# The order of loads and of row groups at a kernel's start, and later weight loads for its last stage: one change to an attention and mixture-of-experts kernel

## The chip, the cores and the metric

The kernel runs on one core of a Trainium2 chip. The metric is the device time of one execution in microseconds, the median of several runs on the chip. Before the change it is 813.06 us, the median of 3 runs (812.66 to 814.68).

## The reference, cut to what matters

```python
# attention: B, H, S, D = 2, 8, 576, 64
psi_rel = log1p(abs(pos[:, None] - pos[None, :]))
x = (psi_rel / log1p(maximum(pos[:, None], 1)))[..., None]
bias = maximum(x @ w1 + b1, 0) @ w2            # 32 hidden units, one bias per head
attn = softmax(q @ k.T / sqrt(D) + bias)       # over keys
x = (attn @ v) as 1152 rows x 512
# first mixture: 4 experts, all of them, weighted by p
x = sum over e of p[:, e] * (maximum(x @ w1[e], 0) @ w2[e])
# second mixture: 8 experts, one for each row
logits = x @ w_gate; e_idx = argmax(logits)
out[mask] = gate_w[mask] * eom[mask, e] * (maximum(x[mask] @ w1[e], 0) @ w2[e])
```

The bias depends on the query row i, the key j and the head, and not on the batch.

## The kernel before

**Engines and order.** Nothing reorders the program: the whole of it is written under a manual schedule, so each engine (TensorE, VectorE, ScalarE, GpSimd) and each DMA queue runs its instructions in the order in which the Python code issues them. Two queues matter here, SP's, which carries most loads, and POOL's, which carries the routing rows of the last stage. Tiles come from pools with a fixed number of buffers; an instruction that writes a buffer waits until the earlier reader of that buffer is done.

**Attention.** The 1152 query rows are nine units of 128: unit u has batch u % 2 and rows from 128 (u // 2), and the ninth has 64 rows of each batch. A head of a unit is one step n of the long loop, n = 8 u + h, 72 steps, each staggered over several turns: `qk(n)` puts scores of 128x576 into PSUM, `soft_max(n)` (L361, VectorE) adds the bias and takes the row extreme in one pass, `soft_exp(n)` (L371, ScalarE) takes the exponential, `e_trans` transposes it, and `av` multiplies with v. The rows call the pass at L361 by its tiles, ns out of sc and bias. `soft_max(n)` for head 0 needs the complete bias tile of its block.

**Bias.** Two units with the same rows share one block of bias, a tile of 128 rows by 8 heads by 576 keys. A block is made in eight groups T of 16 rows: four times `bias_r` (L305 on VectorE or L310 on ScalarE) makes the 32 hidden units for four rows, 128x576; `bias_mm` multiplies them with w2 on TensorE into PSUM; `bias_out` (L332, ScalarE) takes the result out into a buffer bo of SBUF, and one DMA on SP's queue (L335) scatters it into every eighth row of the bias tile. These buffers come from a pool with two under the name bo; the odd groups of block 0 use those of ns instead.

**Keys and values.** k of a batch comes in three loads (`load_k`, a = 0, 1, 2; 512, 512 and 128 KB), is split into two parts by GpSimd in five pieces (`k_split`), and each piece goes through two sets of transposes (`k_trans`, TensorE, PSUM buffers et shared with the transposed exponentials) and two copies (`k_out`, L217). Batch 0 is needed from head 0 on, batch 1 from head 8 on. v is loaded in three parts of a batch; `v_max` (L246) and `v_pow` (L250 to L253) find a power of two over its largest absolute value, `v_scale` (L258 to L260) spreads it and `v_mul` (L264) scales v by it, after which v is split as well.

**The start.** After the first loads a loop over T = 0 to 8 makes block 0; its list `bulk` names the load that is issued behind each bias row. Then come the loads that are left, and the loop over n from -2, which makes the first two groups of block 1 in its first two turns and the transposed k of batch 1 in its turns -1 to 3.

**From the first experts to the second.** The first mixture's matmuls run in 96 tiles (`l1`, `l2`), while the weights of the second are scaled, split and stored to DRAM (wdr). The second mixture works in slots of 128 rows, each with one expert. `route` computes the logits of three units, writes rows of y with their gate to DRAM (ydr, L897, POOL's queue), and `ids_in` (L1011, POOL's queue) gathers the rows of a slot. For the first three slots this is done early, out of units 0 to 5. A slot s then runs through `x_pre` (L1020 on VectorE, then ScalarE), `x_tr` (transposes), `lay1` (L1048) and `lay2` (L1067). `load_e(w, s)` (L1090, SP's queue) fetches the weights of layer w for slot s in four DMAs of 512 KB, with the expert's number in a register. Two buffers for each layer serve slots s % 2.

## Time and profile before

| | |
|---|---|
| median of 3 runs | 813.06 us (812.66 to 814.68) |
| the profiled execution | 816.86 us |
| its span | 815.1 us |
| TensorE busy | 750.1 us, 92% of the span |
| VectorE, ScalarE, GpSimd busy | 488.5, 476.2, 351.7 us |
| granted TensorE clock, mean over the span | 0.971 |
| DMA, mean | 197 GB/s, 160.21 MB |

The profile is one execution, recorded by the hardware. Its page gives busy times of the engines, the span in 40 slices of equal length, the DMA queues, and the costliest groups of instructions; the trace behind it answers for any stretch, line or tile. A granted clock of 1.00 is 2.4 GHz for TensorE and 0.50 is 1.2 GHz. The DMA share is the mean busy share of the core's 16 DMA engines, and can pass 1 by the way in which packets are counted. All times in rows are microseconds from the start of the span, unless marked ns.

### The profile page before, as it was taken

The numbers are of one execution on the slowest core, as the hardware profiler recorded it, in microseconds if no ns is written. First come the engines' busy times: TensorE is split into PE (matmuls) and PEld (weight loads), VectorE is DVE, ScalarE is ACT, GpSimd is POOL, SyncE is SP. The second block draws the span as 40 slices with busy tenths as digits, with TensorE's granted clock in tenths as the row PEclk, the third lists the DMA queues.
The fourth block names the chain that finished last, engine by engine and source line by source line (L and its number), as shares of the span: only waits on it lengthen the run. The fifth ranks groups of instructions, "written<-read, shape, count | busy, mean of one in ns | idle before, by whom it ended". The sixth has DMA issues, their size and how long they took to land. (4 is left out here: it accounts for less than half of the span.)

```text
span 815.1 us, 16401 instructions
## 1 busy us (share of the span) xinstructions
PE 750.1 (92%) x6303; PEld 481.3 (59%) x6303; DVE 488.5 (60%) x1210; ACT 476.2 (58%) x694; POOL 351.7 (43%) x258
## 2 busy tenths in 40 slices
PE   6477999998889999999999999999999789999994
PEld 3245777776785555555555555555555477667771
DVE  6577999998877546565456565465477373333210
ACT  5557999996855657676667667667662132222220
POOL 8532744452553455545546555555543203112110
PEclk9769999999999999999999999999999899999998
DMA  9912443466274386466647468564537739999340
GB/s 210 217 45 70 94 104 99 124 175 137 49 231 153 155 279 245 181 233 232 257 161 273 163 249 277 194 258 142 202 124 291 303 131 341 409 407 360 117 152 16
DMA packets 73860, 160.21 MB, mean 197 GB/s; under 512 B 18928, under 2 KB 27632, under 8 KB 73778
## 3 DMA queue, kind: packets, MB, share of 16 engines
q1 hardware_dynamic: 67904, 144.38, 52.6%
q0 software_dynamic: 4528, 14.47, 5.3%
q8 instruction: 51, 0.84, 0.4%
q10 hardware_dynamic: 1346, 0.28, 0.2%
q14 instruction: 31, 0.25, 0.1%
HBM read 116.35 MB, written 39.34 MB: 191 GB/s over the span
## 5 line engine op out<-in xcount | busy, mean ns | idle before, releaser
L511 POOL TENSOR_TENSOR ring<-wraw,ring 128x1024 f16<-128x1024 f32 x64 | 136.1, 2128 | 119.0 <-ACT wraw L508 103.2
L735 DVE SCALAR_TENSOR_TENSOR h<-hps,h 128x384 f16<-128x384 f32 x96 | 53.2, 557 | 147.4 <-ACT h L734 147.4
L730 PE MATMUL hps<-xt,wt 128*128 128x384 f16 x384 | 126.1, 328 | 2.3 <-DVE h L735 1.8
L731 PE MATMUL hps<-xt,wt 128*128 128x384 f16 x384 | 126.2, 329 | 0.0
L732 PE MATMUL hps<-xt,wt 128*128 128x384 f16 x384 | 125.9, 328 | 0.0
L476 DVE TENSOR_REDUCE wm<-wraw 128x1 f32<-128x1024 f32 x96 | 115.9, 1209 | 0.0
L508 ACT ACTIVATE wraw<-wraw,wR 128x1024 f32<-128x1024 f32 x91 | 104.5, 1148 | 3.0
L747 PE MATMUL yps<-wt,h 128*128 128x512 f16 x264 | 100.1, 379 | 0.0
L748 PE MATMUL yps<-wt,h 128*128 128x512 f16 x264 | 100.1, 379 | 0.0
L749 PE MATMUL yps<-wt,h 128*128 128x512 f16 x264 | 100.1, 379 | 0.0
L734 ACT ACTIVATE h<-hps 128x384 f16<-128x384 f32 x96 | 46.6, 486 | 89.6 <-PE hps L732 85.4
L511 POOL TENSOR_TENSOR wt<-wraw,wt 128x1024 f16<-128x1024 f32 x31 | 66.1, 2132 | 63.8 <-ACT wraw L508 63.4
L503 ACT ACTIVATE ring<-wraw,wR 128x1024 f16<-128x1024 f32 x64 | 73.0, 1141 | 21.5 <-DVE wR L492 18.8
L1048 PE MATMUL l<-xb,wb 128*128 128x128 f16 x1248 | 72.8, 219 | 1.0 <-ACT o L1071 0.8
L1048 PEld LDWEIGHTS <-wb 128*128 128x128 f16 x1248 | 70.7, 98 | 4.6 <-DMA wb<-wdr 1.2
L352 PE MATMUL sc<-kt,qt 128*128 128x288 f32 x320 | 62.4, 320 | 9.1 <-DVE mn L361 6.6
L1067 PE MATMUL l<-wb,xb 128*128 128x512 f16 x312 | 69.5, 379 | 0.8 <-ACT o L1071 0.8
L305 DVE TENSOR_SCALAR_CACHE_REDUCE r<-lm,nbp 128x576 f32<-128x576 f32 x88 | 67.0, 806 | 1.4 <-PE bp L323 1.3
L361 DVE CUSTOM_DVE_ANT_0 ns<-sc,bias 128x576 f32<-128x576 f32 x72 | 54.3, 754 | 21.5 <-PE sc L352 12.5
L1056 DVE SCALAR_TENSOR_TENSOR xb<-l,xb 128x512 f16<-128x512 f32 x26 | 17.6, 691 | 80.2 <-ACT xb L1055 80.2
L1072 POOL DMA_INDIRECT out_x<-o,g x13 | 13.2, 1017 | 106.7 <-ACT o L1071 92.8
L371 ACT ACTIVATE e<-ns,mn 128x576 f32<-128x576 f32 x72 | 56.5, 784 | 1.2 <-DVE mn L361 1.1
(248 smaller groups left out, 1432.9 us busy)
## 6 DMA issues: line engine op xcount, KB each, us to landing
wb<-wdr SPq DMA_DIRECT2D x104, 512.0 KB
wraw<-in_moe_w SPq DMA_DIRECT2D x84, 512.0 KB
wdr<-ring SPq DMA_DIRECT2D x64, 512.0 KB
bias<-bo SPq DMA_DIRECT2D x32, 288.0 KB
wraw<-in_moe_w POOLq DMA_DIRECT2D x12, 512.0 KB, 5.2
qt<-qt SPq DMA_DIRECT2D x40, 128.0 KB
ydr<-y POOLq DMA_DIRECT2D x9, 258.0 KB, 3.6
bias<-bo SPq DMA_DIRECT2D x16, 144.0 KB
```

Source lines behind the costliest of these rows:

```text
L476: dve.tensor_reduce(out=wm[:, w_col(x), k:k + 1], in_=wraw[x][:, k], axis=AX.X, op=ALU.max, apply_absolute_value=True)
L503: act.activation(out=hi, in_=t, func=AF.Copy, scale=R)
L508: act.activation(out=t, in_=t, func=AF.Copy, scale=R)
L511: pool.tensor_tensor(out=lo, in0=t, in1=hi, op=ALU.subtract)
L730: pe.matmul(ps, lhsT=w[:, k, 0, fs], rhs=xt[:, c, 0, k, :], start=(k == 0), stop=False)
L731: pe.matmul(ps, lhsT=w[:, k, 0, fs], rhs=xt[:, c, 1, k, :], start=False, stop=False)
L732: pe.matmul(ps, lhsT=w[:, k, 1, fs], rhs=xt[:, c, 0, k, :], start=False, stop=(k == 3))
L747: pe.matmul(acc[m][t], lhsT=hh, rhs=w[:, f // 2, 0, ws], start=(f == 0), stop=False)
L748: pe.matmul(acc[m][t], lhsT=hh, rhs=w[:, f // 2, 1, ws], start=False, stop=False)
L749: pe.matmul(acc[m][t], lhsT=hl, rhs=w[:, f // 2, 0, ws], start=False, stop=(f == 7))
L1048: pe.matmul(ps[f // 4][:, f % 4, :], lhsT=w[:, k, a, f * 128:f * 128 + 128], rhs=xs[:, b, k, :], start=(k == 0 and f % 4 == 0 and i == 0), ...
L1067: pe.matmul(ps, lhsT=hs[:, a, f, :], rhs=w[:, f // 2, b, c], start=(f == 0 and i == 0), stop=(f == 7 and i == 2))
```

## The change

At the start, the loads of k for batch 1 leave the place ahead of the first bias row and go behind the first and the second; the load of q for unit 1 goes behind the last bias row; the piece of lm (the logarithms) goes from behind the sixth bias row to behind the third, and the v loads of batch 0 from behind the third to fifth to behind the fourth to sixth; the first v load of batch 1 joins the other two, behind all of block 0. The loop over T runs to 10 and makes groups 0 and 1 of block 1 as well, and it scales the low lm piece itself. The maxima of v, their power of two, the scale and the multiplication come one turn later, behind the first `soft_max`. Three of five pieces of k of batch 1 are transposed and copied ahead of the loop over n, the other two in its first two turns.

At the end, only the first layer's weights of slot 0 are fetched where all four sets of the first two slots were; the other three sets are fetched after the third gather, behind a DMA of 16 bytes that reads the third gathered tile.

```diff
@@ the start
-        for a in (2, 0):
-            load_k(1, a)
...
-        bulk = [lambda: load_k(1, 1), lambda: load_q(1), lambda: load_v(0, 0), lambda: load_v(0, 1), lambda: load_v(0, 2),
-                lambda: sp.dma_start(out=lm[:, 0:448], in_=lmc[:, 0:448]), lambda: None, lambda: load_v(1, 0)]
-        for T in range(9):
+        def load_lm():
+            sp.dma_start(out=lm[:, 0:448], in_=lmc[:, 0:448])
+
+        bulk = [[lambda: load_k(1, 2), lambda: load_k(1, 0)], [lambda: load_k(1, 1)], [load_lm], [lambda: load_v(0, 0)],
+                [lambda: load_v(0, 1)], [lambda: load_v(0, 2)], [], [lambda: load_q(1)]]
+        for T in range(11):
             if 3 <= T < 8:
                 for g in range(2):
                     k_out(0, T - 3, g)
-            if T < 8:
+            if T < 10:
                 for tt in range(4):
-                    bias_r(0, T, tt, "a" if tt in AT[T % 2] else "v")
+                    bias_r(T // 8, T % 8, tt, "a" if tt in AT[T % 2] else "v")
+            if T == 7:
+                dve.tensor_scalar(out=lm[:, 0:448], in0=lm[:, 0:448], scalar1=w1c, scalar2=None, op0=ALU.mult)
             if T == 8:
-                for x in range(2):
-                    v_max(0, x)
-                v_pow(0)
                 qk(0)
             if T:
-                bias_mm(0, T - 1)
-                bias_out(0, T - 1, len(AT[(T - 1) % 2]))
-                bulk[T - 1]()
+                x = divmod(T - 1, 8)
+                bias_mm(*x)
+                bias_out(*x, len(AT[(T - 1) % 2]))
+                for f in bulk[T - 1:T]:
+                    for y in f:
+                        y()
...
-        for a in (1, 2):
+        for a in range(3):
             load_v(1, a)
         sp.dma_start(out=cs[:, C_UT:C_N], in_=cst[:, C_UT:C_N])
-        dve.tensor_scalar(out=lm[:, 0:448], in0=lm[:, 0:448], scalar1=w1c, scalar2=None, op0=ALU.mult)
...
+        k_pass(4, 0, 1)
@@ the loop over n
+            if n == -2:
+                for x in range(2):
+                    v_max(0, x)
+                v_pow(0)
-            if n == -2:
+            if n == -1:
                 v_scale(0)
                 v_mul(0)
...
-            if n < 0:
-                for tt in range(4):
-                    bias_r(1, n + 2, tt, "vavv"[tt])
-            if n == 0:
-                rb[1] = 6
...
             if n < 0:
-                bias_mm(1, n + 2)
-                bias_out(1, n + 2, 1)
+                k_pass(n + 4)
...
-            if -1 <= n < 4:
-                k_pass((4, 0, 1, 2, 3)[n + 1])
@@ from the first experts to the second
             if i == 93:
                 for w in range(2):
                     wbuf(w, 0)
-                    load_e(w, 0)
+                load_e(0, 0)
...
         for w in range(2):
             wbuf(w, 1)
-            load_e(w, 1)
...
                     for s in range(NE):
                         ids_in(s)
+                    sp.dma_start(out=after, in_=sl[NE - 1][0][0:1, 0:4])
+                    load_e(1, 0)
+                    for w in range(2):
+                        load_e(w, 1)
```

SP's queue at the program's start. ks and kraw1 are the k loads of batch 1 (the first ks is batch 0's), bias0 a row group of block 0, qt two copies between partitions, q unit 1's rows, vraw parts of v, lm the piece of logarithms. Before:

```order
L184 DMA ks_131<-in_k 64x8x64
L184 DMA ks_133<-in_k 64x8x64
L188 DMA kraw1_135<-in_k 128x8x128
L335 DMA bias0_168<-bo_188 16x8x576
L188 DMA kraw1_135<-in_k 128x8x128
L173 DMA qt_198<-qt_198 64x512
L174 DMA qt_198<-qt_198 64x512
L335 DMA bias0_168<-bo_215 16x8x576
L139 DMA q_219<-in_q 128x8x64
L335 DMA bias0_168<-bo_247 16x8x576
L230 DMA vraw_251<-in_v 128x4x128 x2
```

The same place on SP's queue after the change:

```order
L184 DMA ks_131<-in_k 64x8x64
L335 DMA bias0_164<-bo_184 16x8x576
L184 DMA ks_188<-in_k 64x8x64
L188 DMA kraw1_190<-in_k 128x8x128
L173 DMA qt_197<-qt_197 64x512
L174 DMA qt_197<-qt_197 64x512
L335 DMA bias0_164<-bo_214 16x8x576
L188 DMA kraw1_190<-in_k 128x8x128
L335 DMA bias0_164<-bo_245 16x8x576
L537 DMA lm_117<-in_lmc 128x448
L335 DMA bias0_164<-bo_275 16x8x576
L230 DMA vraw_279<-in_v 128x4x128 x2
```

Each bias row stands ahead of loads that stood ahead of it, and q of unit 1 is gone from this stretch.

VectorE around the first head's pass (L361, ns). r is a row group's hidden units, vm_112, vmx and vpb the maxima of v and their power of two, lm the piece of logarithms that is scaled. Before:

```order
L305 TENSOR_SCALAR r,rmx<-lm,nbp 128x576 x12
L246 TENSOR_REDUCE vm_112<-vraw 128x1 x2
L250 TENSOR_REDUCE vmx<-vm_112 128x1
L251 TENSOR_SCALAR vmx<-vmx 128x1
L252 TENSOR_SCALAR vmx<-vmx 128x1
L253 CAST vpb<-vmx 128x1
L566 TENSOR_SCALAR lm<-lm,cs 128x448
L361 ISA ns,mn<-sc,bias_168 128x576
L361 ISA mn 128x1
```

VectorE in the same place after the change:

```order
L305 TENSOR_SCALAR r,rmx<-lm,nbp 128x576 x12
L549 TENSOR_SCALAR lm<-lm,cs 128x448
L305 TENSOR_SCALAR r,rmx<-lm,nbp 128x576 x6
L361 ISA ns,mn<-sc,bias_164 128x576
L361 ISA mn 128x1
L246 TENSOR_REDUCE vm_112<-vraw 128x1 x2
L250 TENSOR_REDUCE vmx<-vm_112 128x1
L251 TENSOR_SCALAR vmx<-vmx 128x1
L252 TENSOR_SCALAR vmx<-vmx 128x1
L253 CAST vpb<-vmx 128x1
L305 TENSOR_SCALAR r,rmx<-lm,nbp 128x576
```

Six more hidden-unit rows now stand ahead of the first pass, and the maxima of v behind it.

ScalarE before the loop over n, after the change: bo_425 and bo_439 are the results of the first two groups of block 1, kt1 the copies of transposed k of batch 1.

```order
L332 ACTIVATE bo_425<-bp_414,bconst_98,cs_97 128x288
L332 ACTIVATE bo_425<-bp_415,bconst_98,cs_97 128x288
L332 ACTIVATE bo_439<-bp_429,bconst_98,cs_97 128x288
L332 ACTIVATE bo_439<-bp_430,bconst_98,cs_97 128x288
L217 CAST kt1_121<-ktp_460 128x4x64
L217 CAST kt1_121<-ktp_466 128x4x64
L217 CAST kt1_121<-ktp_472 128x4x128
```

Three more such copies follow in the same manner; before the change, all of these stood between exponentials of the loop over n.

SP's queue where the weights of the first two slots are fetched. wb00 is layer 0 of slot 0, wb10 its layer 1; the instructions between are the register arithmetic for an address. Before:

```order
L1090 DMA wb00_7366<-wdr_4102 128x2048
L1090 ISA
L1090 DMA wb10_7380<-wdr_4102 128x2048
L1090 ISA
L1090 DMA wb10_7380<-wdr_4102 128x2048
```

The same place after the change:

```order
L1090 DMA wb00_7367<-wdr_4103 128x2048
L1182 DMA after_4090<-xg_7489 1x4x1
L1090 ISA
L1090 DMA wb10_7368<-wdr_4103 128x2048
L1090 ISA
L1090 DMA wb10_7368<-wdr_4103 128x2048
```

The 16-byte DMA at L1182 reads xg, the third gathered tile, and everything behind it on SP's queue waits with it.

## Rows read from the trace of the kernel before

**Rows 1.** Page: TensorE's busy tenths in 40 slices; DMA total.

```profile
PE   6477999998889999999999999999999789999994
...
DMA packets 73860, 160.21 MB, mean 197 GB/s; under 512 B 18928, under 2 KB 27632, under 8 KB 73778
```

**Rows 2.** Stretches: us, PE, PEld, DVE, ACT, POOL, PEclk, DMA share, GB/s.

```profile
30.00:41.00 11.00, 0.29 (x1) 0.11 (x1) 3.75 (x7) 2.04 (x4) 1.95 (x2) 0.54 1.09 208
41.01:80.06 39.05, 29.09 (x237) 19.11 (x238) 29.38 (x71) 25.31 (x46) 10.52 (x11) 0.81 0.24 60
```

**Rows 3.** Timeline, VectorE: start, duration, what, [idle before <-releaser].

```profile
35.84 1.35 DVE L246 TENSOR_REDUCE vm<-vraw 128x1 f32<-128x1152 f32 x1 [4.22 <-DMA bias<-bo]
...
37.23 0.15 DVE L250 TENSOR_REDUCE vmx<-vm 128x1 f32<-128x2 f32 x1
...
41.01 0.76 DVE L361 CUSTOM_DVE_ANT_0 ns<-sc,bias 128x576 f32<-128x576 f32 x1 [2.64 <-DMA bias<-bo]
...
43.55 0.81 DVE L305 TENSOR_SCALAR_CACHE_REDUCE r<-lm,nbp 128x576 f32<-128x576 f32 x1
44.28 0.81 DVE L305 TENSOR_SCALAR_CACHE_REDUCE r<-lm,nbp 128x576 f32<-128x576 f32 x1
...
80.06 0.75 DVE L361 CUSTOM_DVE_ANT_0 ns<-sc,bias 128x576 f32<-128x576 f32 x1
```

**Rows 4.** Waits of VectorE, 41.00 to 80.06: us, times, longest.

```profile
DVE ns L361 <- PE sc L352: 3.3, 1, 3.3
DVE ns L361 <- ACT e L371: 2.6, 2, 1.6
DVE vP L258 <- PE vpp L257: 2.2, 1, 2.2
DVE r L305 <- PE bp L323: 1.3, 1, 1.3
```

**Rows 5.** Timeline, DMA issues and times to landing of the gather chain.

```profile
626.60 1.62 POOL L897 DMA_DIRECT2D ydr<-y  x3 [10.43 <-DVE y L895]
637.67 1.10 POOL L1011 DMA_INDIRECT xg<-ydr,ids_e  x1 [9.46 <-DVE oh L849]
...
ydr<-y POOLq DMA_DIRECT2D x4, 258.0 KB, 7.3
ydr<-y POOLq DMA_DIRECT2D x9, 258.0 KB, 3.6
DMA to landing us min/median/max: 3.9/6.5/7.0
...
644.25 0.69 DVE L1020 TENSOR_REDUCE g<-xg 128x1 f32<-128x512 f32 x1 [3.46 <-DMA xg<-ydr,ids_e]
646.79 1.89 PE L836 MATMUL lgp<-wgt,yt 128*128 128x16 f32 x8 [4.95 <-ACT yt L831]
662.57 2.85 PE L1048 MATMUL l<-xb,wb 128*128 128x128 f16 x48
```

**Rows 6.** Stretches of the gather chain and behind, columns as in rows 2.

```profile
640.00:646.00 6.00, 1.84 (x11) 0.87 (x9) 2.19 (x11) 0.65 (x2) 2.06 (x5) 0.95 1.03 405
645.46:652.28 6.82, 5.49 (x21) 3.67 (x22) 2.38 (x17) 1.21 (x3) 0.18 (x1) 0.51 0.18 71
680.00:760.00 80.00, 79.05 (x904) 58.58 (x902) 25.16 (x70) 20.89 (x35) 16.52 (x23) 1.00 0.93 370
```

**Rows 7.** Timeline, SP's queue at the start: issue, duration, what.

```profile
4.60 2.03 SPq L184 DMA_DIRECT2D ks<-in_k  x2
...
12.22 0.60 SPq L335 DMA_DIRECT2D bias<-bo  x1
```

**Rows 8.** DMA view: packets in 12 to 41 us, then 5 to 9.

```profile
DMA packets 8425, 6.13 MB, mean 211 GB/s; under 512 B 1945, under 2 KB 7143, under 8 KB 8423
...
DMA packets 2494, 1.14 MB, mean 284 GB/s; under 512 B 500, under 2 KB 2494, under 8 KB 2494
```

**Rows 9.** Timeline, ScalarE: the copies of one k piece.

```profile
67.86 1.15 ACT L217 CAST kt<-ktp 128x512 fp32r<-128x512 f32 x2 [1.06 <-PE ktp L208]
```

More of the change, by code (lines that the diff above doesn't have):

```diff
@@ L782, in attn_moe_moe_kernel @@
     tab = rt_p.tile([1, 128], I32, name="tab")
+    after = rt_p.tile([1, 4], F32, name="after")
     early = rt_p.tile([1, NE], I32, name="early")
```

## Prediction, made before the changed kernel was run

> **What bounds the kernel now.** I read the page's slices first. TensorE is at 9 tenths or more nearly everywhere; the thin places are the first four slices (to about 80 us), a shallow dip around 200 us, and the two slices from 632 to 672 us [rows 1]. The diff acts in two of them: the start, and the step from the first expert layer to the second.
>
> The table by stretches prices the start [rows 2]. From 30 to 41 us it is busy 0.29 of 11.00 at a granted clock of 0.54, while the DMA share is 1.09 and 208 GB/s move: the DMA engines are full and everything else waits. What it waits for stands in VectorE's rows [rows 3]: the first head's maximum at 41.01 sat 2.64 us for a bias row, because it needs all eight bias rows of block 0. From it to the ninth head's maximum 39.05 us pass (41.01 to 80.06). In that stretch VectorE is busy 29.38 us and TensorE 29.09 at a clock of 0.81 [rows 2]; VectorE's 9.67 idle us are split between score matmuls, exponentials, the v scale and bias matmuls [rows 4].
>
> The second thin place is a chain. The three ydr stores are issued from 626.60; the gathers behind them start only at 637.67, after 9.46 us of waiting; the first gathered rows arrive at 644.25, where VectorE has sat 3.46 us; TensorE, idle 4.95 us for a copy that ScalarE makes behind these rows, goes on at 646.79 [rows 5]. For the next 6.82 us the granted clock is 0.51, that is the 1.2 GHz level, with TensorE busy 5.49. SP's weight loads fill the DMA engines meanwhile: 405 GB/s from 640 to 646 [rows 6].
>
> **The profiled execution against the median.** It took 816.86 us (span 815.1 plus 1.8 around it), 3.80 above the median of 813.06. No term below is a share of the whole, so savings read from it are taken off 813.06 as they stand.
>
> **Part 1, the order of the loads: +1.5 us on the last bias row.** Ahead of the last row of block 0 the change puts 128 + 512 KB of k that before were issued from 4.60 on, ahead of the first bias row at 12.22 [rows 7]. It takes out q of unit 1, 256 KB. The v loads of batch 0 all stay ahead of it, and so does the lm piece; each bias row moves past one v load only. Net 384 KB, 0.39 MB, more before the row that ends the wait. At the mean of 211 GB/s of 12 to 41 us this is 1.9 us, at the 284 GB/s of the k loads 1.4 [rows 8]. I take 1.5. Bounds: -1.2 (q's 0.26 MB at 211 GB/s gone, and the k pieces hidden in a gap) to 3.1 (0.66 MB of k at 211 GB/s with nothing given back). POOL splits these k pieces after all of batch 0, in the order of before, so it comes to them late and I count nothing there.
>
> **Part 2, what fills the wait.** Two bias groups of block 1 go from after the first maximum to before it: 6 instructions on VectorE, each 0.73 from start to start (43.55 to 44.28) [rows 3], 4.4 us less in the stretch. The absolute maxima of v and their power of two go the other way: two reductions of 1.35 (35.84) and four small ones of 0.15 (37.23 is the first) [rows 3], 3.3 us more. Busy time falls from 29.4 to 28.3. The scaling of the low lm piece only moves to an earlier place in the wait.
>
> The groups' two matmul sets, their ScalarE evictions and the copies of three of five k pieces leave the stretch too. A k piece is 8 transposes on TensorE and two ScalarE copies, 1.15 together [rows 9]; two pieces stay, but come before the first transposed exponentials. The matmuls and k copies stand behind a catch: the eviction of the second group writes a buffer from which row 6 of block 0 must first have left. ScalarE waits there until one row before the end, and the six copies queue behind it, with the score matmul of head 1 behind their transposes on TensorE. VectorE covers this: after the first maximum it has the v maxima and one more bias row, 3.3 + 0.7 us of its own.
>
> The idle time in the stretch: of the 9.4 us in [rows 4] the 3.3 for scores (the first k piece and a bias group stood in front of them at 1.2 GHz) should fall to 1, the 2.6 for exponentials to 0.5, the 1.3 for bias matmuls to 0; the v scale of batch 1 keeps about 1.5 of its 2.2, and the same wait for batch 0, which the 30 to 41 us stretch hid, now costs about 1. That is 4.0, an estimate. The stretch becomes 28.3 + 4.0 = 32.3 for 39.05, 6.7 less; minus the 1.5 of part 1: **5.2 us**. Bounds: with 1.0 idle and the same delay 8.2; with all 9.67 idle still there and 3.1 of delay, -2.0 (a loss). Behind the ninth head TensorE stands at 9 tenths [rows 1] and every later stage starts from the heads, so this goes through to the end.
>
> **Part 3, the late weights: 5.0 us.** Three of four weight loads of the first two slots (12 DMAs of 512 KB) leave their place on SP ahead of the gathers and are issued after the third gather has landed, behind a 16-byte DMA that reads it. Without them the stores meet an idle queue: a store takes 7.3 us to land in that stretch, 3.6 over the whole program, and a gather 6.5 in the median where the quickest takes 3.9 [rows 5]. The last store then lands near 632, the gathers are issued at about 632.4, 633.8 and 635.1 (the offsets of before), and land at 636 to 639. VectorE reaches the first at 644.25 - 3.46 = 640.79, so its whole wait goes and the chain behind it, ScalarE and TensorE, moves up by 3.46. What is late next is that chain itself: 2.5 us from VectorE's start to TensorE's (644.25 to 646.79), which leaves TensorE 1.5 idle. With 1.5 instead of 4.95 idle the clock may stay at 2.4 GHz; 5.49 busy us at the lower level are worth at most 2.7, and VectorE's routing steps hold some of it, so 1.5, bounds 0 and 2.7. Sum 3.5 + 1.5 = 5.0, bounds 3.5 and 6.2.
>
> The price of delay: 12 x 0.524 = 6.3 MB at 405 GB/s are 15.5 us from about 639, the end near 655. Slot 1's first layer starts at 662.57 [rows 5] less 5.0 = 657.6; its 2 MB stand second in the queue and have landed by 651. The margin of some 6 us hides the change; SP's next loads wait for TensorE to free their buffers anyway.
>
> A rule speaks against this part: the Trainium skill, page "DMA: Bandwidth & Descriptors", section "Rules for kernel authors", says to issue a DMA early, compute, and wait on its semaphore late. By it, moving 12 loads back by some 15 us would be a loss; the trace shows the other side of it, a gather that lands at 644.25 behind loads that are needed 10 us later. The rule's result is the second rival.
>
> **Rivals.** *The start gives nothing* (chance 0.13): the last rows land 3 us later, ScalarE's wait for the buffer holds the copies, and the first heads idle as before. For it: DMA sets the start, and the change removes only 0.26 MB from it; against it: VectorE's own work covers some 4 us. 813.06 - 5.0 = 808.1.
>
> *The late weights cost what the gather gains* (0.09): the wait for rows becomes a wait for weights in slot 1's first layer. It decides when 4.2 MB from 641 take longer than to 657.6, under 253 GB/s; at the page's mean for the whole program, 197 [rows 1], they take 21 us, TensorE waits near 5 us and part 3 is nil. 813.06 - 5.2 = 807.9. Against it: 405 GB/s in the same stretch with the same DMAs [rows 6].
>
> *The change does not do what it says* (0.06): the rows land 3 later and the waits stay, and weights are late too. Within 2.4 us of 813.1.
>
> *Slower* (0.04): the moved 6.3 MB land in the stage of the slots, where the DMA share is 0.93 from 680 to 760 us [rows 6]. If that queue does not drain before slot 2's weights are due, TensorE waits in slot after slot for up to all that those loads take, 15.5 us: 813.06 - 5.2 - 5.0 + 15.5 = 818. It decides when the part of it that no margin covers passes 12.6 us. Against it: TensorE is busy 79.05 of 80 there, so loads are ahead.
>
> **How the numbers follow.** Forecast (0.68): 5.2 + 5.0 = 10.2 off 813.06, 802.9; alone it spans 799.1 (8.2 and 5.8) to 807. The range 799.0 to 808.4 takes in the first two rivals. A measurement of this kernel tells about 0.3%, 2.4 us, from no change: faster by more is the forecast and two rivals, 0.90; within it 0.06; slower 0.04.
>
> **What would show it.** Right: the first maximum 1 to 3 us after 41.0; the ninth near 75 for 80.06, with VectorE idle 3 to 5 us between them; bias groups of block 1 on VectorE before the first maximum; the first gather issued near 632; no wait of VectorE for it; a granted clock of 1.00 behind it; no wait of the slot matmuls for weights over 1 us. Wrong: a first maximum after 45, an idle sum of 9, a gather still issued after 635, or TensorE waiting for weights at the first layer of slot 1.

## The result, and the profile after

The changed kernel takes 805.57 us, the median of 5 runs (803.55 to 810.10), where the kernel before took 813.06 in 5 runs (811.46 to 814.68). The ratio is 0.9913, interval 0.9888 to 0.9938, that is 5.0 to 9.1 us faster. The forecast was 802.9 in a range of 799.0 to 808.4: the direction and the two main mechanisms held, one term (the clock behind the gather) came only in part, and the size came out 2.7 us too large.

| | before | after |
|---|---|---|
| median | 813.06 us | 805.57 us |
| profiled execution, and its span | 816.86, 815.1 us | 805.57, 803.8 us |
| first and ninth head's pass on VectorE | 41.01, 80.06 us | 42.49, 74.00 us |
| third gather issued, counted from the first ydr store of its three | 640.41 - 626.60 = 13.8 us | 627.82 - 619.75 = 8.1 us |
| last matmul row of the routing chain (L836) | 646.79 us | 636.37 us |

TensorE's busy tenths on the page of the changed kernel, in 40 slices:

```profile
PE   6677999998889999999999999999998989999994
```

Against [rows 1], the second slice went from 4 to 6 tenths, and the thin place near the end from 7 and 8 to 8 and more.

The table by stretches of the changed kernel: us, then busy us (and instructions) of PE, PEld, DVE, ACT, POOL, then granted clock, DMA share, GB/s. The first row is the wait before the first head's pass, the second goes from that pass to the ninth, the third is the end of the routing chain:

```profile
30.00:42.49 12.49, 4.03 (x41) 1.63 (x42) 4.19 (x12) 4.63 (x10) 1.75 (x2) 0.79 1.07 180
...
42.49:74.00 31.51, 23.53 (x203) 18.30 (x204) 28.08 (x67) 22.96 (x41) 10.48 (x11) 0.87 0.42 97
...
637.90:641.40 3.50, 3.50 (x13) 1.83 (x12) 2.12 (x14) 0.59 (x1) 0.00 (x0) 0.51 1.01 392
```

The stretch over the first nine heads is 31.51 us long for 39.05 in [rows 2], and VectorE is busy 28.08 of it for 29.38: its idle time fell from 9.67 to 3.43. The wait ahead of it still moves data at a full DMA share. Here is VectorE around its end, in the timeline (start, duration, what, and in brackets the idle time before it with what ended it):

```profile
28.09 1.48 DVE L549 TENSOR_SCALAR lm<-lm,cs 128x448 f32<-128x448 f32 x1 [0.87 <-DMA lm<-in_lmc]
...
33.37 0.81 DVE L305 TENSOR_SCALAR_CACHE_REDUCE r<-lm,nbp 128x576 f32<-128x576 f32 x1
...
42.49 0.76 DVE L361 CUSTOM_DVE_ANT_0 ns<-sc,bias 128x576 f32<-128x576 f32 x1 [8.30 <-DMA bias<-bo]
...
43.17 2.61 DVE L246 TENSOR_REDUCE vm<-vraw 128x1 f32<-128x1152 f32 x2
...
47.74 0.76 DVE L361 CUSTOM_DVE_ANT_0 ns<-sc,bias 128x576 f32<-128x576 f32 x1 [0.47 <-PE sc L352]
...
74.00 0.75 DVE L361 CUSTOM_DVE_ANT_0 ns<-sc,bias 128x576 f32<-128x576 f32 x1
```

The bias groups of block 1 are done at 34.2, and then VectorE sits 8.30 us for the last bias row: the wait is as much of a wait as before, but it now comes after work that used to come behind it. VectorE's waits between 30 and 80 us (total, times, longest):

```profile
DVE ns L361 <- DMA bias<-bo: 8.3, 1, 8.3
DVE ns L361 <- PE sc L352: 1.3, 2, 0.8
DVE vP L258 <- PE vpp L257: 0.9, 1, 0.9
DVE etl L390 <- ACT eth L384: 0.8, 1, 0.8
```

Against [rows 4], the 3.3 for a score matmul became 1.3 in two, the waits for exponentials and for bias matmuls are gone, and of the 2.2 for the v scale 0.9 is left; a wait of 0.8 for ScalarE's transposed exponentials (L390) is new. ScalarE's timeline shows the catch that the prediction named:

```profile
34.59 1.07 ACT L332 ACTIVATE bo<-bp,bconst,cs 128x288 f32<-128x288 f32 x2 [2.52 <-DMA bias<-bo]
41.01 1.07 ACT L332 ACTIVATE bo<-bp,bconst,cs 128x288 f32<-128x288 f32 x2 [5.35 <-DMA bias<-bo]
41.97 0.65 ACT L217 CAST kt<-ktp 128x256 fp32r<-128x256 f32 x2
```

The two evictions of block 1's groups wait 2.52 and 5.35 us for a buffer, and the first k copy starts only at 41.97.

At the end, the gather chain of the changed kernel, from the timelines of GpSimd, VectorE and TensorE; the third row, from the view of L1011, is the time from a gather's issue to its landing:

```profile
619.75 1.63 POOL L897 DMA_DIRECT2D ydr<-y  x3 [10.58 <-DVE y L895]
625.08 1.11 POOL L1011 DMA_INDIRECT xg<-ydr,ids_e  x1 [3.71 <-issue]
...
DMA to landing us min/median/max: 3.6/3.6/3.6
...
633.84 0.67 DVE L1020 TENSOR_REDUCE g<-xg 128x1 f32<-128x512 f32 x1
...
636.37 1.06 PE L836 MATMUL lgp<-wgt,yt 128*128 128x16 f32 x8 [1.37 <-ACT yt L831]
...
642.05 1.50 PE L1048 MATMUL l<-xb,wb 128*128 128x128 f16 x24
```

In [rows 5] the first gather came 11.07 us behind the stores and VectorE sat 3.46 us for its rows; now it comes 5.33 us behind them, and VectorE does not wait. The profile puts the 9.46 us of [rows 5] down to a VectorE row (L849); that is a coincidence in time, since the same row starts at 630.23 in the changed kernel, 5 us behind the gather. What the gather reads are the rows that the ydr stores write, so the wait is for these stores to land (7.3 us in the median, [rows 5]). TensorE's idle time ahead of L836 fell from 4.95 to 1.37 us. SP's queue in the same stretch shows the DMA of 16 bytes and the weight loads behind it:

```profile
631.46 0.74 SPq L1182 DMA_DIRECT2D after<-xg  x1
632.42 32.02 SPq L1090 DMA_DIRECT2D wb<-wdr  x19
```

### The profile page after: what moved, and what is told of

Read it like the earlier page. It is cut to its first block, busy times and chain, and to the rows that moved or that the text cites. A ratio compares the mean times of both kernels' runs of the same rounds, so it can differ in the third digit from the quotient of the medians.

```text
span 803.8 us, 16406 instructions
## 1 busy us (share of the span) xinstructions
PE 746.6 (93%) x6303; PEld 479.8 (60%) x6303; DVE 489.1 (61%) x1210; ACT 476.7 (59%) x694; POOL 352.2 (44%) x258
## 5 line engine op out<-in xcount | busy, mean ns | idle before, releaser
L361 DVE CUSTOM_DVE_ANT_0 ns<-sc,bias 128x576 f32<-128x576 f32 x72 | 54.3, 754 | 21.7 <-PE sc L352 9.6
```

## The experiments

Each kernel ran beside the kernel before. The first four rows of the table were run on one chip, the next four and the last four on others; the medians of the kernel before there are 814.09, 814.65 and 814.11 us. A ratio is always to the kernel before on the same chip; it is formed from all the runs and is not the quotient of the two medians. Passes and stretches are read from one trace of each kernel.

| kernel | median us | ratio, interval | first, ninth pass us |
|---|---|---|---|
| late weights alone | 810.95 | 0.9944 (0.9919 to 0.9968) | 41.27, 79.23 |
| start alone | 811.19 | 0.9955 (0.9931 to 0.9980) | 42.43, 74.63 |
| whole change, old order of work | 812.08 | 0.9965 (0.9940 to 0.9990) | 42.66, 79.95 |
| whole change, k loads early | 802.30 | 0.9843 (0.9810 to 0.9875) | 38.12, 69.06 |
| whole change, no waiting DMA | 812.29 | 0.9970 (0.9948 to 0.9992) | 42.69, 74.62 |
| whole change, k pieces in the loop | 811.19 | 0.9959 (0.9942 to 0.9976) | 42.21, 79.09 |
| k early, v behind block 0 | 802.36 | 0.9848 (0.9826 to 0.9870) | 34.46, 71.09 |
| whole change again | 806.03 | 0.9891 (0.9869 to 0.9913) | 43.82, 76.22 |
| whole change, bias groups in the loop | 815.42 | 1.0008 (0.9985 to 1.0032) | 42.89, 82.20 |
| k early, k copies first | 800.65 | 0.9833 (0.9808 to 0.9858) | 38.22, 69.05 |
| k early, q and then v behind block 0 | 798.72 | 0.9805 (0.9774 to 0.9836) | 34.53, 67.93 |
| k early again | 801.25 | 0.9837 (0.9811 to 0.9862) | 38.64, 70.89 |

### The two halves apart

Late weights alone: the three hunks at the end, on the kernel before.

> Before with the end's part of the change alone: three of the four weight loads of the first two slots behind the third gather. Theory (both parts pay and add up; the two traces put some 7.0 us into the start and 4.3 us into the end, of 11.3 in all, while the medians differ by 7.5): 3 to 5 us faster than before, ratio 0.994 to 0.996; the first gather is issued some 5 us earlier, VectorE does not wait for the gathered rows and TensorE waits 1 to 2 us for the copy instead of 4.95. Rival (all of the measured 7.5 us is the start, and the later weights cost what the gather gains): within 1 us of before, with a wait for weights in the first layer of slot 1.

Start alone: the rest of the change.

> Before with the start's part of the change alone: the order of loads and of work, weights as before. Theory: the rest of the 7.5 us, 3 to 5 us faster, ratio 0.994 to 0.996; the ninth head's pass near 74 us, some 6 us earlier than in the profile of before, which was itself a long execution by 3.8 us. Rival (the start gives its full 7.0 us, and the end gives nothing in the median): ratio 0.991, equal to the whole change.

Ratios 0.9944 and 0.9955: 4.6 us (2.6 to 6.6) for the end and 3.7 us (1.6 to 5.6) for the start. Both intervals leave out 1, so neither half is empty and both rivals fall. The sum, 8.2 us, agrees with the 7.1 of the first comparison (0.9913) and the 8.9 of the second (0.9891). By the medians alone the halves are 3.1 and 2.9 us, so neither is known better than its interval. In the trace of late weights alone L836 waits 1.37 us, as in the whole change. (The expectation counts the trace pair as 7.0 and 4.3; why 11.3 is more than any comparison of medians gives stands in the next section.)

### What pays at the start: loads or work

The new order of loads and the late weights, but groups, maxima of v and k pieces in their old places.

```diff
-        for T in range(11):
+        for T in range(9):
...
             if T == 8:
+                for x in range(2):
+                    v_max(0, x)
+                v_pow(0)
                 qk(0)
...
-        k_pass(4, 0, 1)
```

> The whole change but for the order of work at the start: loads in the new order and late weights, while the first two groups of block 1, the maxima of v and the k copies stand where they stood before. Theory (what pays at the start is work moved into the wait, the loads alone only shift the last bias row): first head's pass within 1.5 us of 41 to 42.5 us, and the time within 1.5 us of the kernel with late weights alone, some 3 to 4 us slower than the whole change. Rival (the order of loads pays by itself): within 1 us of the whole change.

It came out at 0.9965, against 0.9944 for late weights alone on the same chip: the new order of loads by itself gives nothing, its first pass is 1.4 us later and the ninth stands at 79.95. The rival falls. (In this kernel the maxima of v stand ahead of the first pass and wait 8.75 and 2.93 us for v, which now comes later; the first pass follows them without a wait, at 42.66 where the changed kernel has it at 42.49.) So the start gains only with the work that was moved into the wait. That work with all loads in their old order was not run; at the least it needs the earlier lm piece, which VectorE scales at 28.09 after a wait of 0.87 us for it. Two runs take the work apart.

The k pieces back in the loop over heads:

```diff
-        k_pass(4, 0, 1)
...
-            if n < 0:
-                k_pass(n + 4)
...
+            if -1 <= n < 4:
+                k_pass((4, 0, 1, 2, 3)[n + 1])
```

> The whole change, but the transposes and copies of batch 1's k stand in the loop over heads again, where they stood before (turns -1 to 3). It parts the work moved at the start: bias groups against k pieces. Theory (the k pieces are part of the gain: three pieces of 8 transposes and 1.15 us of ScalarE leave the first heads): 1.5 to 3 us slower than the changed kernel. Rival (the bias groups are all of it, since ScalarE's copies stood behind its wait for an output buffer until 41 us and filled nothing): within 0.8 us of the changed kernel.

0.9959 beside 0.9891 for the whole change on the same chip, and 5.2 us slower by the medians: more than the theory asked for. The waits of VectorE in this kernel between 42 and 80 us:

```profile
DVE ns L361 <- ACT bo L332: 9.1, 1, 9.1
DVE ns L361 <- ACT e L371: 4.8, 2, 2.8
DVE vP L258 <- PE vpp L257: 2.2, 1, 2.2
DVE ns L361 <- ACT vz L269: 1.4, 1, 1.4
```

The first lies in front of the stretch and ends at the first pass, at 42.21 for 42.49; I read it as the wait for the last bias row, as after the change, though the profile names ScalarE's eviction, which ended just before, as what released it. Of the others, the 2.2 for the v scale is that of [rows 4] exactly and the wait for exponentials is larger (4.8 for 2.6); the waits for scores and for bias matmuls are not back, and one for ScalarE's split of v is new. VectorE is busy 28.02 us between the first and the ninth pass, as after the change (28.08), and still the stretch is 36.88 us instead of 31.51. So it was not VectorE's work that made the difference here, but what ScalarE and TensorE had to do between two heads. (The profiled execution took 814.59 us, 3.4 above this kernel's median, so its waits may be on the large side.) I then expected that the groups would not matter at all.

The two bias groups back in the loop:

```diff
-        for T in range(11):
+        for T in range(9):
...
             if n < 0:
+                bias_mm(1, n + 2)
+                bias_out(1, n + 2, 1)
                 k_pass(n + 4)
```

(and their `bias_r` in the turns -2 and -1, as before).

> The whole change, but the two bias groups of block 1 stand in the loop over heads again, as before; the k pieces and the v steps stay where the change puts them. Theory (after the run with the k pieces in the loop, 5.2 us slower than the changed kernel: the k pieces are all that pays at the start, and VectorE's work moved into the wait pays nothing, because VectorE was not what the first heads waited for): within 1.5 us of the changed kernel, first to ninth pass 31 to 33 us. Rival (both moves are needed; the groups are 4.4 us of VectorE): 2.5 to 4.5 us slower, first to ninth pass 34 to 36 us.

This theory fell, and the rival's figure is passed as well: 1.0008, 9.4 us over the 806.03 of the whole change (7.7 by its other ratio, 0.9913), with the late weights in it. First to ninth pass is 39.31 us. TensorE's timeline in this kernel:

```profile
43.71 1.33 PE L352 MATMUL sc<-kt,qt 128*128 128x288 f32 x4 [9.59 <-DVE mn L361]
47.72 3.60 PE L323 MATMUL bp<-r,cs 128*32 128x288 f32 x16 [2.68 <-DVE r L305]
51.24 1.81 PE L208 MATMUL ktp<-cs,kraw 128*128 128x128 f32 x8
52.89 0.22 PE L257 MATMUL vpp<-idb,vpb 128*128 128x128 bf16 x1
52.92 0.78 PE L352 MATMUL sc<-kt,qt 128*128 128x288 f32 x4
```

And ScalarE's:

```profile
50.39 0.59 ACT L332 ACTIVATE bo<-bp,bconst,cs 128x288 f32<-128x288 f32 x1 [14.30 <-PE bp L323]
51.35 0.59 ACT L332 ACTIVATE bo<-bp,bconst,cs 128x288 f32<-128x288 f32 x1 [0.37 <-PE bp L323]
52.39 1.32 ACT L217 CAST kt<-ktp 128x512 fp32r<-128x512 f32 x2 [0.45 <-PE ktp L208]
53.59 0.78 ACT L371 ACTIVATE e<-ns,mn 128x576 f32<-128x576 f32 x1
```

The maxima of v stand behind the first pass now (the change put them there), so a group that follows them gets its last row on VectorE only at 48.31; its matmuls run 3.60 us at the lower level of TensorE's clock (granted clock 0.50 from 47.72 to 51.32, and 0.76 from the first pass to the ninth, for 0.87 after the change); the eviction waits 14.30 us for them at the head of ScalarE's queue; and the first head's exponential, whose input was ready at 43.7, starts at 53.59. The third head's pass came at 58.68 for 51.85. So both moves are needed, and neither has a price of its own: against the whole change at 0.9891, undoing the k pieces costs 5.5 us, the groups 9.5, and undoing both with the maxima of v in front again 6.0; against 0.9913 it is 3.7, 7.7 and 4.2. No run has the groups in the wait and the maxima of v ahead of the first pass, so what the move of the maxima is worth alone is open.

### Where the k loads stand

The whole change, with the two k loads of batch 1 ahead of the first bias row as before:

```diff
         for a in (0, 1, 2):
             load_k(0, a)
+        for a in (2, 0):
+            load_k(1, a)
...
-        bulk = [[lambda: load_k(1, 2), lambda: load_k(1, 0)], [lambda: load_k(1, 1)], [load_lm], [lambda: load_v(0, 0)],
+        bulk = [[], [lambda: load_k(1, 1)], [load_lm], [lambda: load_v(0, 0)],
```

> The whole change, but with the two k loads of batch 1 (640 KB) ahead of the first bias row again, where DMA stood part idle after the change (share 0.68 in the first 12 us for 0.98). Theory (they are nearly free there): the first head's pass 1.5 to 3 us earlier than 42.5, and the time 1 to 2.5 us under the changed kernel. Rival (the queue holds the same bytes ahead of the last row either way, and what is late next is the wait of ScalarE for its output buffer): first pass and time within 1 us of the changed kernel.

> The kernel with early k itself, for comparison on the same chip: ratio to before 0.982 to 0.987.

Ratios 0.9843 and 0.9837: 4 to 6 us under the changed kernel, more than either theory said. The first 12 us of the changed kernel:

```profile
0.00:12.00 12.00, 4.98 (x22) 2.31 (x22) 6.15 (x18) 4.35 (x8) 9.48 (x17) 1.00 0.68 165
```

And of the kernel with early k:

```profile
0.00:12.00 12.00, 4.77 (x26) 2.14 (x30) 5.95 (x16) 4.37 (x9) 9.26 (x17) 1.00 0.98 219
```

The change left the DMA engines idle for nearly a third of this stretch (share 0.68), because nothing was queued between k of batch 0 and the first bias row; with early k they are full (0.98). Up to the first pass both kernels move 8.0 MB, early k at a mean share of 1.00 and the changed kernel at 0.93: the bytes that could have moved in the first 12 us stand later ahead of the last bias row. The first pass comes at 38.12 instead of 42.49, 4.4 us earlier (3.9 to 5.7 between the two traces of each kernel), and with 30.94 us from it to the ninth pass, for 31.51 after the change, all of it reaches the heads (32.25 and 32.40 in the second traces).

### The buffer that ScalarE waits for

Early k, with the k splits, transposes and copies ahead of the second group's matmuls and eviction:

```diff
+            if T == 10:
+                for a in (4, 0, 1, 2, 3):
+                    k_split(1, a)
+                k_pass(4, 0, 1)
             if T:
                 x = divmod(T - 1, 8)
...
-        k_pass(4, 0, 1)
```

> The kernel with early k, and the transposes and copies of three k pieces ahead of the second group's matmuls and eviction, so that ScalarE copies while the buffer is not yet free (it waited 5.0 us with the six copies behind it). Theory (the prediction's: VectorE's own work after the first pass covers that wait): within 1 us of the kernel with early k. Rival (the wait is on the path of the first heads): 1.5 to 3 us faster than it, ninth pass at 66 to 67.5 for 69.06.

The edit did what it should. ScalarE in this kernel:

```profile
31.57 0.63 ACT L217 CAST kt<-ktp 128x256 fp32r<-128x256 f32 x2
32.75 1.12 ACT L217 CAST kt<-ktp 128x512 fp32r<-128x512 f32 x2 [0.55 <-PE ktp L208]
34.53 1.17 ACT L217 CAST kt<-ktp 128x512 fp32r<-128x512 f32 x2 [0.66 <-PE ktp L208]
36.82 1.07 ACT L332 ACTIVATE bo<-bp,bconst,cs 128x288 f32<-128x288 f32 x2 [1.11 <-DMA bias<-bo]
```

The copies fill the wait, of which 1.11 us is left (5.03 with early k alone), and the time stays: 0.9833 beside 0.9837, the ninth pass at 69.05 beside 69.06 in the first trace of early k and 70.89 in its second. VectorE's work behind the first pass covers this wait, as the prediction said.

### What is late next when the rows come early

Early k, and v of batch 0 behind the last bias row, its steps one turn later:

```diff
-        bulk = [[], [lambda: load_k(1, 1)], [load_lm], [lambda: load_v(0, 0)],
-                [lambda: load_v(0, 1)], [lambda: load_v(0, 2)], [], [lambda: load_q(1)]]
+        bulk = [[], [lambda: load_k(1, 1)], [load_lm], [], [], [], [],
+                [lambda: load_v(0, 0), lambda: load_v(0, 1), lambda: load_v(0, 2), lambda: load_q(1)]]
...
-            if n == -2:
+            if n == -1:
                 for x in range(2):
                     v_max(0, x)
```

> The changed kernel with the two k loads ahead of the first bias row again, and with the v loads of batch 0 behind the last bias row of block 0 (their maxima, scale and split one turn later). Theory (the first head waits for every byte queued ahead of the last bias row, at some 200 GB/s): 1.15 MB less ahead of it, so the last row lands 4 to 5.5 us earlier, the first pass stands near 33 to 34 us for 38.1; v itself is late next, so 2 to 4 us of this reach the end: 798 to 800.5 where the kernel with early k takes 802.3. Rival (the heads are held by v or by ScalarE's wait for its output buffer, whatever the first pass does): within 1 us of the kernel with early k.

The first pass came at 34.46, 3.7 us earlier and near what was expected, and nothing of it was left at the ninth (71.09 for 69.06) or at the end (0.9848, where the two runs of early k gave 0.9843 and 0.9837). Waits of TensorE in this kernel between 30 and 72 us:

```profile
PE qtp L159 <- POOL qs L147: 4.4, 1, 4.4
PE sc L352 <- DVE mn L361: 4.4, 3, 2.3
```

The first is the transposes of unit 1's q, waiting for GpSimd, which splits q only behind the late v; the granted clock over the nine heads is 0.77 here, for 0.89 and 0.82 in the two traces of early k. Moving q and its split ahead of v removes this wait:

```diff
-                [lambda: load_v(0, 0), lambda: load_v(0, 1), lambda: load_v(0, 2), lambda: load_q(1)]]
+                [lambda: load_q(1), lambda: load_v(0, 0), lambda: load_v(0, 1), lambda: load_v(0, 2)]]
...
+            if n == -1:
+                split_q(1)
```

> The kernel with v behind the last bias row, and now q of unit 1 ahead of v on SP's queue and its split ahead of v's on GpSimd. In the former run TensorE waited 4.4 us for that split, and the ninth pass came at 71.09 although the first came at 34.46. Theory (this queueing behind late v ate the gain): ninth pass at 66.5 to 68.5, and 1 to 2.5 us faster than the kernel with early k. Rival (the scale of v, for which ScalarE waited 4.0 us, holds the heads as well): ninth pass at 69.5 to 71, no faster than early k.

TensorE's waits between 30 and 72 us are now these, and the granted clock over the nine heads is 0.90:

```profile
PE sc L352 <- DVE mn L361: 6.6, 6, 2.3
PE vpp L257 <- DVE vpb L253: 1.0, 1, 1.0
```

The ninth pass stands at 67.93, and the time is 798.72, ratio 0.9805 (0.9774 to 0.9836): the lowest median of this study, 15.4 us under the kernel before on its chip. Against early k alone (0.9837) it is 2.5 us, the size that was expected, but the intervals overlap, so this gain is not shown. Of the 4.1 us by which the first pass is earlier than in the second trace of early k (34.53 for 38.64), 3.0 reach the ninth; against the first trace 1.1 of 3.6 do. ScalarE still waits for the scale of v, 4.6 us, and the ninth pass is 3.2 us earlier than in the run before, so that wait was not what held it at 71.09. Whether it is part of why the stretch takes 33.40 us, longer than the 30.94 and 32.25 of early k, is open.

### The DMA that waits for the gather

The whole change without the 16-byte DMA:

```diff
-                    sp.dma_start(out=after, in_=sl[NE - 1][0][0:1, 0:4])
                     load_e(1, 0)
```

> The whole change without the 16-byte DMA that reads the third gathered tile; the three sets of weight loads stand at their later place in SP's order. Theory (what pays at the end is that no weight load is in flight while the ydr stores and the gathers are; the DMA that waits is what keeps them back, since SP runs far ahead of the others): the loads are issued some 15 us earlier, the gathers land as late as before, VectorE waits for the rows again, and the time is 2.5 to 4.5 us above the changed kernel, at ratio 0.9955, that of the start's part alone. Rival (the later place in SP's order is enough): within 1 us of the changed kernel.

0.9970, 6.3 us over the 806.03 of the whole change (0.9891), more than the theory's 4.5 (4.6 against the other ratio, 0.9913), and within the interval of the start's part alone (0.9931 to 0.9980): the end's gain is gone. SP's weight loads, GpSimd's first gather and VectorE's first use of its rows in this kernel (its line numbers are one lower):

```profile
611.77 44.38 SPq L1089 DMA_DIRECT2D wb<-wdr  x20
...
630.98 1.10 POOL L1010 DMA_INDIRECT xg<-ydr,ids_e  x1 [9.30 <-DVE oh L848]
...
637.51 0.69 DVE L1019 TENSOR_REDUCE g<-xg 128x1 f32<-128x512 f32 x1 [3.27 <-DMA xg<-ydr,ids_e]
```

Waits of 9.30 and 3.27 us stand where [rows 5] has 9.46 and 3.46, and the three gathers take 6.4 to 6.5 us to land, for 3.6. The later place in SP's order does nothing by itself, since SP runs ahead of the other engines: it issues all 16 weight loads of the first two slots between 611.77 and 632 here, where in the changed kernel 12 of them start only at 632.42. From 625 to 632 the DMA engines move 398 GB/s in this kernel; from 620 to 632 they move 133 GB/s in the changed one. The wait for a landed gather is what keeps the weights off the DMA engines. The rival falls.

The last run of the whole change gave the second comparison and the second trace named above.

> The changed kernel itself, for comparison on the same chip. Ratio to before 0.989 to 0.994; first pass near 42.5 us, ninth near 74, first gather issued 10 us behind the first ydr store of its group or less, no wait of VectorE for gathered rows in the first slot.

Its ratio, 0.9891, is in the range; its first pass, 43.82, is 1.3 us later than in the first trace and the ninth, 76.22, is 2.2 later than expected, so one trace of the start does not hold to better than about 2 us.

## Why the prediction was right, and where its size was off

**Part 1, +1.5 us on the first pass.** It came 1.48 us later (42.49 for 41.01), and 1.2 to 2.8 in the other kernels of the table with these loads (42.21 to 43.82). The net was right, but its two terms were both too small, so that it came out to a tenth of a microsecond is luck: the prediction counted bytes at the DMA's rate, at most 3.1 us of k against 1.2 of q. With early k the first pass is 2.4 to 2.9 us earlier than before (38.64 and 38.12), so the rest of the change gave back that much, and the k loads cost 4.4 us (3.9 to 5.7), not 3.1. The k loads stood ahead of the last bias row before the change too; to count them as additional bytes is right only because the queue runs dry without them in the first 12 us (the share falls by 0.30, which is 3.6 us of DMA time), and the prediction did not say so. It thought of a gap only as something that might hide the k loads in their new place; it was their old place that hid them. On the other side it counted q alone. Before the change SP also issued four loads of batch 1's v from 33.21 on, while the last bias rows were on their way; now they stand behind the rows of block 1 on SP's queue and go out only after the first pass (at 42.69, and at 38.46 with early k). That these bytes are the rest of the 2.4 to 2.9 us is likely and not shown.

**Part 2, 39.05 to 32.3 us.** Measured 31.51; VectorE busy 28.08 for 28.3, idle 3.43 for 4.0. In the trace of the start alone it is 32.20. What the sum could not tell is which move pays: it priced the groups at 4.4 us of VectorE's work and the k pieces as some idle time, and the runs with one of them undone cost 7.7 to 9.5 and 3.7 to 5.5. With engines that each run in order, an instruction at the wrong place in one queue stops the others, and the busy time that it takes is the smaller part.

**The start, 5.2 us net.** The ninth pass is 6.06 us earlier in the pair of traces. The kernel with late weights alone, which has the old start, has it at 79.23; the four kernels with the changed start (after, again, start alone, no waiting DMA) have it at 74.00, 76.22, 74.63 and 74.62, on average 74.87. Against the mean of 80.06 and 79.23 that is 4.8 us, and the run of the start alone gives 3.7 (1.6 to 5.6). So the term was probably a little too large; 5.2 lies within that interval.

**Part 3, 3.5 + 1.5 us.** By the two traces: L836 starts 10.42 us earlier (646.79 to 636.37), of which 7.02 were there at the first mixture's tile that starts at 608.40 before and at 601.38 after; so 3.40 for the wait. The first slot's first layer starts 11.35 earlier (653.40 to 642.05), so 0.93 for the clock, where 1.5 was forecast: the step that failed is "the clock may stay at 2.4 GHz", and with it the sign "a granted clock of 1.00 behind it". It did not stay: behind an idle time of only 1.37 us the granted clock was 0.51 from 637.90 to 641.40, with TensorE busy all 3.50 us; what was gained is 3.50 us at the lower level instead of 6.82. (The 6.82 us began at 645.46, 1.33 us ahead of the row at 646.79; the prediction counted them as behind it.) From L836 to the first slot's first layer the kernels with late weights take 5.7 us in three traces (the change, again, late weights alone), those without 6.4 to 6.7 (before, start alone, no waiting DMA). The rest of the chain held in detail: first gather forecast at 632.4 on the old time scale, 625.08 + 7.02 = 632.1 measured; landing 3.6 us each for 6.5; TensorE's idle time 1.37 for 1.5. The price of delay was nil as said: between 600 and 690 us the trace of the changed kernel has no wait for weights, and that of late weights alone one of 0.3 us.

A rule of the Trainium skill spoke against this part (page "DMA: Bandwidth & Descriptors", section "Rules for kernel authors": issue a DMA early, compute, and wait on its semaphore late). At the end of this kernel the opposite paid, 4.6 us (2.6 to 6.6) with late weights alone, since early bulk loads stood in the way of a short transfer that was needed at once. At the start the rule held: k issued early, into a queue that is dry otherwise, is worth 4 to 6 us.

**The whole, 10.2 us.** Measured: 7.5 by the first medians, 5.0 to 9.1 by the interval of that ratio, 7.1 to 10.7 by that of the second. The pair of traces shows 11.3, and that is too much for a reason that can be seen: 6.06 at the ninth pass and 4.3 at the end belong to the change, but 1.0 appears between the forty-ninth pass and the last (179.35 to 240.57 before, 173.33 to 233.54 after), where the change does nothing. Late weights alone has the old instructions there, and takes 40.86 us from the forty-first pass to the fifty-seventh where the trace of before takes 42.79 (and four others, with the same instructions there, 41.95 to 42.52), and 12.15 from the last pass to ScalarE's eviction of an early expert tile (at 249.81 and 254.15) for 13.58: 3.4 us between two executions of the same instructions. In the second of these places TensorE's granted clock was 0.56 from 249.00 to 252.70 in the trace of before. That trace was 3.80 us above its median, and some of that can lie there. No term of the sum was read from these stretches, so taking the savings off 813.06 as they stand did little harm; the miss is in the two terms, 5.2 for 3.7 to 4.8 and 5.0 for 4.3 to 4.6. They make 8.0 to 9.4 together, and what is left between that and 7.5 is within the interval and is not settled. The ends that the prediction gives the forecast alone do not follow from its bounds: the low one takes 5.8 for part 3 where its bound is 6.2, which would be 798.7, and the bounds of a loss at the start, -2.0, and of part 3, 3.5, would make the high one 811.6 and not 807.

**The rivals.** That the start gives nothing fell with the run of the start alone; that late weights cost what they gain, with late weights alone; that nothing happens or that it gets slower, with the result. The stage of the slots was busy 79.52 of 80 us from 680 to 760, for 79.05 in [rows 6].

## What to carry to other kernels

Count the bytes ahead of the transfer that ends a wait, and also the time in which the queue has nothing to move: a load that is moved out of an empty stretch costs its whole time later. When work is moved into a wait, move whole chains, on all engines; half of it left behind at the head of an in-order queue can cost more than the whole did. Bulk loads that are needed later can be kept off the DMA engines by a few bytes that read the tile of the urgent transfer: their place in the program alone does not do it.

## What the runs showed of the hardware that was not expected

The three gathers landed in 3.6 us each when no weight loads had been issued since 614.3, and in 6.5 to 6.6 us in the kernel before, with weight loads in flight (405 GB/s, [rows 6]). TensorE's granted clock was 0.51, the 1.2 GHz level, from 637.90 to 641.40 in the changed kernel, behind an idle time of only 1.37 us and 1.5 us of work; in the kernel before it was 0.51 for 6.82 us, from inside an idle time of 4.95 us on [rows 6].
